# A gated mix of sliding-window attention and SwiGLU: values held in TensorE's four column strips while the exponentials stream

## Chip, cores and metric

One Trainium2 chip, one of its cores. The metric is the device time of one execution in microseconds (us), a median over runs. A profile is one execution, taken on its own.

## The reference, cut to what matters

Two branches over the same 2048 tokens of 512 numbers, mixed by a gate for each token: causal attention with a window of 256 keys and 32 heads of 16 numbers, and a SwiGLU feed-forward layer of width 1376. All inputs are bf16.

```python
qkv = (x @ wqkv).reshape(B, S, 3, H, Dh).transpose(2, 0, 3, 1, 4)   # H = 32, Dh = 16, S = 2048
q, k, v = qkv[0], qkv[1], qkv[2]
scores = jnp.einsum("bhqd,bhkd->bhqk", q, k) * (Dh ** -0.5)
mask = (idx[:, None] - idx[None, :] >= 0) & (idx[:, None] - idx[None, :] < 256)
p = softmax(jnp.where(mask, scores, -1e9))
a = jnp.einsum("bhqk,bhkd->bhqd", p, v).transpose(0, 2, 1, 3).reshape(B, S, D) @ wo
b = (silu(x @ w1) * (x @ w3)) @ w2
g = sigmoid((x * gate_w).sum(-1, keepdims=True))
out = g * a + (1 - g) * b
```

## The kernel before

**Order.** Nothing runs in source order. Every piece of work is an operation of a `Plan`, with an engine, an expected duration, inputs, a due time and the buffers that it takes and frees. `Plan.emit` (L62) is a list scheduler: it takes the engine that can start first, and among the operations that could start then the one that is due first; the instructions are then written out in that order. The attention stage's due times come from `at(c, t)`, which spreads 4 blocks of 16 steps over `TA` = 234.3 from `T0` = 11.49 (L292); the feed-forward's are spread evenly from `TF0` to `TF1` (L642). These numbers order the work and are no measurements. Each engine executes its list in order.

**Layout.** `xT` holds x transposed, 512 numbers in four chunks of 128 partitions. Attention runs in four blocks `c` of 8 heads (128 channels). A block's channels are four groups `s` of 32, two heads each; `a` or `h` names the head of a pair.

**Projections** (`projections`, L364): for each block and 512 tokens, K and Q as four 512-column matmuls each (L381), V as 128-column matmuls (L439). K is kept twice in `kbd`, each copy with the other head's rows set to zero by a multiplication with `rowsA`: in block 0 by VectorE and ScalarE out of PSUM (L390, L395), in the others by GpSimd out of the copy `kt` (L402, L405). A score tile so has 64 keys of head 0 and the same 64 keys of head 1 on its 128 partitions. V goes to `vbd` in four copies of half the partitions, two by ScalarE (L447) and two by VectorE (L449); each group's 34 columns are 16 values and a one for either head, with zeros elsewhere.

**Scores** (`main_batch`, L488, and `far_batch`, L515): a batch is 8 matmuls of 32 rows, in four row strips of TensorE, into `su`, four PSUM banks of which there is one set. ScalarE takes the exponentials of all four banks in one instruction (L505, L547, L553) into `E`. The diagonal is masked by VectorE (L486), the far edge of the window by GpSimd (L559). The pieces at the far edge of eight 64-key tiles are one batch.

**P times V** (`pv`, L576): for each 128 queries, a 128x128 piece of `E` is the weight and 34 columns of `vbd` stream, up to six pieces for each of four groups (L595). The result has the queries on partitions, 16 numbers and the sum beside them for each head. VectorE inverts the sums (L603), multiplies by them and by the gate `gq` (L606) into `oc`, and a transposing DMA on SP's queue (L612) writes it into `OT`.

**Output** (`output`, L795): four matmuls over `OT` and `wo` (L804), VectorE adds the feed-forward branch `bsb` (L816), which carries the factor 1 - g, and SP stores the row (L821). The last half row is summed on TensorE instead, by an identity matmul (L808).

**Feed-forward** (L658 on): gate and up matmuls (L712), a tanh on ScalarE (L722), two products on VectorE (L726, L732), the down matmuls (L773) and their eviction (L778).

**Start** (`opening`, L262): constants, 27 warm-up matmuls, x, then the weights, in the order in which they are issued; `landed` (L294) is when the plan expects them. x's first 512 tokens are transposed by TensorE (L319), the rest by transposing DMAs (L249). PSUM holds `su` and four banks `ch`, which everything else shares.

Of the kernel before, what the change touches and what calls it, by code (L numbers as in the profile page):

```python
# [13 lines left out]
DH = 16  # L14
# [7 lines left out]
class Op:  # L22
    __slots__ = ("eng", "dur", "lat", "fn", "deps", "due", "take", "free", "seq", "end", "slots")

    def __init__(self, eng, dur, fn, deps, due, take, free, lat, seq):
# [3 lines left out]
        self.end = None  # L29

# [8 lines left out]
class Plan:  # L39
# [22 lines left out]
    def emit(self):  # L62
# [14 lines left out]
        while ready:  # L77
# [21 lines left out]
            est, op = min(rows, key=lambda r: (r[1].due, r[1].seq))  # L99
# [25 lines left out]
def kernel(  # L125
# [27 lines left out]
    NKB = S // KB  # L153
    HALF = (0, 2, 4)
# [4 lines left out]
    ps = ctx.enter_context(tc.tile_pool(name="ps", bufs=1, space=bass.MemoryType.PSUM))  # L159

# [17 lines left out]
    kbd = pp.tile([P, NKB, 2, KB], BF16, name="kbd")  # L178
    qT = pp.tile([P, S + KB], BF16, name="qT")
    vbd = pp.tile([P, NKB, 4, 2 * (DH + 1)], BF16, name="vbd")  # L180
# [9 lines left out]
    mdiag = pp.tile([P, KB], BF16, name="mdiag")  # L190
    E = [pp.tile([P, 4, 4, 2, 384], BF16, name=f"E_{i}") for i in range(2)]
# [3 lines left out]
    oc = [pp.tile([P, 8, DH], BF16, name=f"oc_{i}") for i in range(8)]  # L195
    rden = [pp.tile([P, 8, 1], F32, name=f"rden_{i}") for i in range(8)]
# [3 lines left out]

    plan = Plan({"su": 1, "ch": 4, "E": 2, "kt": 2, "tt": 2, "h1": 2,
                 "oc": 8, "ot": 4, "hT": 1})
    add = plan.add


# [18 lines left out]
    def constants3():  # L224
        nc.gpsimd.memset(qT[:, S:S + KB], 0.0)
        nc.gpsimd.memset(mdiag[:], BIG)
        for lo in (0, KB):
            nc.gpsimd.affine_select(out=mdiag[lo:lo + KB, :], in_=mdiag[lo:lo + KB, :],
                                    pattern=[[1, KB]], compare_op=ALU.is_ge, fill=0.0,
                                    base=0, channel_multiplier=-1)  # L230

    def constants4():
        nc.gpsimd.memset(hb[:], 0.0)
        for e in E:
            nc.gpsimd.memset(e[:].rearrange("p t s a q -> p (t s) a q")[:, :, 0, 320:384], 0.0)
        v5 = vbd[:].rearrange("p k s (a d) -> p (k s) a d", a=2)
        nc.vector.memset(vbd[:, 0:NKB // 2], 0.0)
        nc.vector.memset(vbd[:, NKB // 2:NKB], 0.0)
        nc.gpsimd.memset(v5[0:KB, :, 0, DH:DH + 1], 1.0)
        nc.gpsimd.memset(v5[KB:P, :, 1, DH:DH + 1], 1.0)  # L240
# [21 lines left out]
    def opening():  # L262
# [10 lines left out]
        for b in (1, 0, 2):  # L273
            load_w(wqkv_sb, A_wqkv, b * D, b * D + 2 * P)
# [601 lines left out]
```

## Time and profile before

| | |
|---|---|
| median of 3 runs (lowest, highest) | 251.43 us (251.09, 251.58) |
| span of the profiled execution, first to last instruction | 249.4 us |
| TensorE busy | 244.4 us, 3483 matmuls |
| VectorE busy | 187.4 us |
| ScalarE busy | 185.4 us, of which L505 112.6 |
| GpSimd busy | 109.2 us, of which L559 65.0 and L405 37.6 |
| granted clock of TensorE, mean | 0.998 |
| first and last score batch start | 14.1 us and 236.7 us |

The span is what the engines did; the time of a run also has what lies before the first and behind the last instruction. A row of a group says which line, engine and operation, out<-in by the program's names, the shapes and how many; then the busy time and the mean in ns of one; then how long the engine stood idle just before them and what ended most of that. PE is TensorE, PEld its weight loads, DVE VectorE, ACT ScalarE, POOL GpSimd, and SPq the queue of SyncE that issues DMAs. A matmul's own duration includes its way through the array, so that matmuls overlap; the distance between the starts of two of them is what each takes of TensorE's line.

### The profile page before, as it was taken

Reading aid. Unit: us, or ns where it says so; the run is one execution under the profiler, and the core shown is the slowest. Engines: PE = TensorE matmul, PEld = TensorE weight load, DVE = VectorE, ACT = ScalarE, POOL = GpSimd, SP = SyncE. Lnnn points to the kernel's source line nnn. Section 1 sums busy time; section 2 is a strip of 40 time slices with the busy share of each in tenths; the row PEclk is TensorE's granted clock in tenths of the full one; section 3 lists DMA queues with packets and bytes.
Section 4 is the critical chain, followed back from the end, with each engine's and each line's share of the span. In section 5 each row is a group of like instructions: output and inputs, shape, how many; then the busy total and the mean of one; then the engine's idle time right before and its main releaser. Section 6 shows DMA issues by size and latency. Waiting matters only on the chain.

```text
span 249.4 us, 8138 instructions
## 1 busy us (share of the span) xinstructions
PE 244.4 (98%) x3483; PEld 133.8 (54%) x3483; DVE 187.4 (75%) x409; ACT 185.4 (74%) x186; POOL 109.2 (44%) x102
## 2 busy tenths in 40 slices
PE   8999999999999999999999999999999999999994
PEld 8645555555564554645464655555465554644462
DVE  5687888658878868757777988765787988787662
ACT  3377989688888887767888798776698877886631
POOL 8002945060318366475335717474344715470300
PEclk9999999999999999999999999999999999999999
DMA  6998951000000010100000010000000111211112
GB/s 202 314 253 251 230 136 25 16 8 13 13 5 18 13 26 11 20 8 11 13 8 18 5 25 19 20 5 13 13 5 18 29 38 45 61 50 54 51 53 75
DMA packets 30652, 13.67 MB, mean 55 GB/s; under 512 B 19896, under 2 KB 30616, under 8 KB 30616
## 3 DMA queue, kind: packets, MB, share of 16 engines
q1 hardware_dynamic: 29920, 12.70, 22.1%
q8 instruction: 27, 0.44, 0.8%
q10 hardware_dynamic: 696, 0.46, 0.6%
q14 instruction: 9, 0.07, 0.1%
HBM read 6.85 MB, written 2.10 MB: 36 GB/s over the span
## 4 chain that ended last, share of the span: by engine, by line
PE 94%; DVE 2%; DMA 1%; ACT 1%; issue 0%; SPq 0%; DVEq 0%
PE ch L712 29%; PE ch L773 15%; PE ch L595 15%; PE ch L381 11%; PE su L500 8%; PE ch L439 6%; PE ch L804 5%; PE su L532 2%; PE su L260 1%; DVE E L486 1%; DMA OT<-oc 1%; PE ch L672 1%; ACT E L505 1%; PE ch L319 1%; DVE oc L606 0%
## 5 line engine op out<-in xcount | busy, mean ns | idle before, releaser
L505 ACT ACTIVATE E<-su 128x2048 bf16<-128x2048 f32 x60 | 112.6, 1877 | 28.7 <-PE su L500 27.8
L559 POOL TENSOR_SCALAR_AFFINE_SELECT E<-E 64x1024 bf16<-64x1024 bf16 x56 | 65.0, 1161 | 84.7 <-ACT E L547 82.3
L712 PE MATMUL ch<-xT,w_sb 128*128 128x512 bf16 (+1 forms) x328 | 79.5, 375 | 0.0
L595 PEld LDWEIGHTS <-E 128*128 128x128 bf16 x1440 | 43.9, 96 | 12.8 <-issue 3.0
L405 POOL TENSOR_SCALAR kbd<-kt,rowsA 128x512 bf16<-128x512 bf16 x24 | 37.6, 1578 | 27.3 <-DVE kt L402 23.3
L595 PE MATMUL ch<-vbd,E 128*128 128x34 bf16 x1440 | 46.6, 178 | 0.5 <-DVE E L486 0.3
L712 PEld LDWEIGHTS <-w_sb 128*128 128x128 bf16 x328 | 28.3, 98 | 29.8 <-issue 3.6
L486 DVE TENSOR_TENSOR E<-E,mdiag 128x512 bf16<-128x512 bf16 x64 | 34.8, 544 | 9.1 <-ACT E L505 7.7
L773 PE MATMUL ch<-w_sb,hT 128*128 128x512 bf16 x160 | 41.3, 379 | 0.0
L726 DVE SCALAR_TENSOR_TENSOR h<-tt,ch 128x512 bf16<-128x512 bf16 (+1 forms) x44 | 30.1, 684 | 6.4 <-ACT tt L722 5.7
L381 PE MATMUL ch<-xT,wqkv_sb 128*128 128x512 bf16 x128 | 33.9, 379 | 0.0
L547 ACT ACTIVATE E<-su 128x2048 bf16<-128x2048 f32 (+1 forms) x16 | 26.6, 1663 | 8.9 <-PE su L532 6.5
L722 ACT ACTIVATE tt<-ch 128x512 bf16<-128x512 f32 (+1 forms) x44 | 26.0, 596 | 6.8 <-PE ch L712 6.3
L732 DVE SCALAR_TENSOR_TENSOR hT<-h,ch 128x512 bf16<-128x512 bf16 x40 | 27.5, 687 | 3.8
L603 DVE RECIPROCAL rden<-ch 128x8 f32<-128x8 f32 x64 | 13.1, 205 | 19.4 <-PE ch L595 18.8
L606 DVE SCALAR_TENSOR_TENSOR oc<-ch,gq,rden 128x128 bf16<-128x128 f32 x64 | 22.5, 351 | 2.3
L500 PE MATMUL su<-qT,kbd 32*128 32x256 bf16 x480 | 23.8, 273 | 0.0
L773 PEld LDWEIGHTS <-hT 128*128 128x128 bf16 x160 | 13.1, 97 | 13.0 <-issue 1.9
L500 PEld LDWEIGHTS <-kbd 32*128 32x128 bf16 x480 | 7.1, 92 | 22.1 <-issue 20.8
L439 PEld LDWEIGHTS <-xT 128*128 128x128 bf16 x256 | 15.5, 97 | 4.6 <-issue 1.5
L804 PE MATMUL ch<-wo_sb,OT 128*128 128x512 bf16 (+1 forms) x68 | 16.6, 367 | 0.3 <-DMA OT<-oc 0.3
L381 PEld LDWEIGHTS <-wqkv_sb 128*128 128x128 bf16 x128 | 10.7, 97 | 11.2 <-issue 1.7
(70 smaller groups left out, 167.8 us busy)
## 6 DMA issues: line engine op xcount, KB each, us to landing
out_dram<-ot SPq DMA_DIRECT2D x15, 128.0 KB, 1.9
wqkv_sb<-in_A_wqkv_dram SPq DMA_DIRECT2D x6, 256.0 KB, 5.3
w_sb<-in_B_w_dram SPq DMA_DIRECT2D x1, 1280.0 KB, 6.5
w_sb<-in_B_w_dram SPq DMA_DIRECT2D x2, 608.0 KB, 6.5
w_sb<-in_B_w_dram SPq DMA_DIRECT2D x2, 512.0 KB, 5.5
OT<-oc SPq DMA_TRANSPOSE x64, 2.3
wo_sb<-in_A_wo_dram SPq DMA_DIRECT2D x1, 512.0 KB, 5.0
xs<-in_A_x_dram SPq DMA_DIRECT2D x1, 256.0 KB, 2.8
```

What stands on the lines that cost most here:

```text
L381: nc.tensor.matmul(pst[:], lhsT=wqkv_sb[:, dc, col + c * P:col + (c + 1) * P], rhs=xT[:, dc, tq * 512:(tq + 1) * 512], start=(dc == 0), st ...
L405: nc.gpsimd.tensor_scalar_mul(out=kv[:, :, h, :], in0=kt[kj.at["kt"]][:].rearrange("p (k t) -> p k t", t=KB), scalar1=rowsA[:, h:h + 1])
L439: nc.tensor.matmul(pst[:, mm * w:(mm + 1) * w], lhsT=xT[:, dc, m * P:(m + 1) * P], rhs=rhs, start=(dc == 0), stop=(dc == NDC - 1))
L486: nc.vector.tensor_tensor(out=e, in0=e, in1=mdiag[:, None, :].to_broadcast([P, 8, KB]), op=ALU.min)
L500: nc.tensor.matmul(su[:, s, par * 256:(par + 1) * 256], lhsT=kbd[r, 2 * t + par, :, :].rearrange("p a k -> p (a k)"), rhs=qT[r, q0:q0 + 25 ...
L505: nc.scalar.activation(out=E[ej.at["E"]][:, t % 4, :, :, 0:256], in_=su[:].rearrange("p s (a q) -> p s a q", a=2), func=ACT.Exp, scale=SCALE)
L559: nc.gpsimd.affine_select(out=e[lo:lo + KB], in_=e[lo:lo + KB], pattern=[[0, 16], [-1, KB]], compare_op=ALU.is_ge, fill=0.0, base=-1, chan ...
L595: nc.tensor.matmul(po[:, 34 * s:34 * s + 34], lhsT=e[:, off:off + P], rhs=vbd[:, 2 * t + par, s, :], start=(bi == 0), stop=(bi == len(bloc ...
L712: nc.tensor.matmul(ch[job.at["ch"]][:, t0:t1], lhsT=wA[:, dc, :] if joint else w[:, dc, f * P:(f + 1) * P], rhs=xT[:, dc, tcb * 512 + t0:t ...
L726: nc.vector.scalar_tensor_tensor(out=h1[job.at["h1"]][ru, :], in0=tt[job.at["tt"]][rg, :], scalar=1.0, in1=ch[job.at["ch"]][rg, :], op0=AL ...
L773: nc.tensor.matmul(bps[:], lhsT=ht[:, mm * P:(mm + 1) * P], rhs=w2_sb[0:fs, f, :], start=(f == 0), stop=(f == NFC - 1))
L804: nc.tensor.matmul(pso[:, 0:part], lhsT=OT[:, c, m * P:(m + 1) * P], rhs=wo_sb[:, c, n0:n1], start=(c == 0), stop=(c == NDC - 1))
```

## The change

- **P times V is turned round.** V is the weight: 128 keys by 32 columns (16 values, the sum's column and padding) for one head, in one of four column strips of TensorE, one for each group of heads. The exponentials stream, up to 256 columns at a time. The two heads of a pair are two chains in two PSUM banks. `pv` runs for 512 queries at once: it waits for all their masks, and the result has channels on partitions, as `OT` needs them, without a transpose.
- **Scores are tiled by 128 keys of one head** (`head_keys`): 8 matmuls per main batch as before, over the 256 queries that start 64 behind the tile. The first 64 queries and the last 64 of four tiles are an edge batch. K has three copies: `kz` (zeros around the other head, `[h1 | h0 | h0 | h1]` by halves) and `k1`.
- **Masks**: GpSimd masks two 64x512 pieces per main batch (`near`, `far`), VectorE an edge batch in four instructions.
- **V** is copied out of PSUM by VectorE twice, and GpSimd makes four half copies of it for the edge tiles.
- **Softmax sums**: two DMAs gather them into `den`, VectorE inverts, two DMAs spill them to HBM, one spreads each over 16 partitions, four merge the second head's rows into `raw`; one product on VectorE writes `OT`. The gate moves to the output's eviction.
- **Start**: the first 512 tokens' K and Q weights are loaded ahead of w1 and w3, and K and Q come as two half chains each, where gate and up did before.
- **Order**: new due times (`K`), and ScalarE holds itself free for an exponential that will be ready soon (`hold`, negative here).

The core of the diff; flags beginning with `_` choose between placements, and `_pv` and `_vs` are set, `_km`, `_nm`, `_lo` are not.

```diff
-    T0, TA, TF0, TF1 = 11.49, 234.3, -7.168, 250.6
+    K = {"T0": 5.107, "TA": 219.856, "TF0": -3.263, "TF1": 261.659, "PV": -1.916, "EDGE": 1.036, "HOLD": -4.141, "LEAD": 11.653, ...}
+            held = [r for r in lists[eng] if r[1].hold and r[0] <= first + r[1].hold]
+            est, op = min(held or rows, key=lambda r: (r[1].due, r[1].seq))
...
+    vs = pp.tile([P, 2 * DH + 2, 3 * NV], BF16, name="vs")
+    Em = [pp.tile([P, 4, 2, 256], BF16, name=f"Em_{i}") for i in range(9)]
+    Ee = [pp.tile([P, 4, 4, 2, KB], BF16, name=f"Ee_{i}") for i in range(2)]
...
         load_x(0, 2, nc.sync)
         load_x(2, 4, nc.scalar)
-        load_w(w1_sb, B_w1, 0, 2 * P, True)
+        load_w(wqkv_sb, A_wqkv, D, D + 2 * P, True)
         nc.scalar.dma_start(out=gwr[:], in_=gate_w.rearrange("(c p) -> c p", p=P))
+        load_w(wqkv_sb, A_wqkv, 0, 2 * P)
+        load_w(w1_sb, B_w1, 0, 2 * P)
         load_w(w3_sb, B_w3, 0, 2 * P)
...
+            k_ready[(c, tq)] = [add("DVE" if K["_km"] else "POOL", 0.3 if K["_km"] else 1.6, lambda h=h: kmask(h), [b] + war, due, free=[(kj, "kt")])
+                                for h in range(3)]
...
+            def v_all(a, v_from=v_from, v_of=v_of):
+                nc.vector.tensor_copy(out=v_of(slice(0, P), 0, a), in_=v_from(slice(0, P), a))
+                    nc.gpsimd.tensor_copy(out=v_of(to, base, 0), in_=v_of(half, 0, 0))
+                nc.gpsimd.tensor_copy(out=v_of(rows, base, 1), in_=v_of(rows, 0, 1))
...
+            q0 = P * t + KB
+            for a in range(2):
+                for s in range(4):
+                    nc.tensor.matmul(su[:, s, a * 256:(a + 1) * 256], lhsT=head_keys(r, t, a),
+                                     rhs=qT[r, q0:q0 + 256], start=True, stop=True)
+        def near():
+            e = Em[job.at["Em"]][KB:P, :, :, 0:KB].rearrange("p s a q -> p (s a) q")
+            nc.gpsimd.affine_select(out=e, in_=e, pattern=[[0, 8], [1, KB]], compare_op=ALU.is_ge, fill=0.0,
+                                    base=0, channel_multiplier=-1)
...
+    def pieces_of(w):
+        q0, q1 = 512 * w, 512 * w + 512
+        res = []
+        for t in range(max(0, 4 * w - 2), 4 * w + 4):
+            lo, hi = max(q0, P * t + KB), min(q1, P * t + 320)
+            res.append(("main", t, lo, hi))
+            if t >= 4 * w:
+                res.append(("lo", t, P * t, P * t + KB))
+            if t < 4 * w + 2 and P * t + 320 < S:
+                res.append(("hi", t, P * t + 320, P * t + 384))
+        return res
+                for s in range(4):
...
+                    nc.tensor.matmul(po[32 * s:32 * s + 32, lo - 512 * w:hi - 512 * w],
+                                     lhsT=vs[:, 2 * a:2 * a + 32, i], rhs=mov, start=(n == 0),
+                                     stop=(n == len(todo) - 1), skip_group_check=True)
...
+        def gather(a):
+            (nc.scalar if final and a else nc.sync).dma_start(out=den[64 * a:64 * a + 64, :],
+                              in_=raw[DH - a:P:32, a, :].rearrange("p (r q) -> p r q", q=32))
+        def invert():
+            nc.vector.reciprocal(out=rden[:], in_=den[:])
+        def spill(a):
+            (nc.scalar if final and a else nc.sync).dma_start(out=hbm[:, a, :].rearrange("s (r q) -> s r q", q=32), in_=rden[64 * a:64 * a + 64, :])
+        def spread():
+            src = hbm[:].rearrange("s a q -> (s a) q")
+            nc.sync.dma_start(out=rec[:], in_=src[:, None, :].to_broadcast([8, DH, 512]))
+        def merge(s):
+            rows = slice(32 * s + DH, 32 * s + 32)
+            (nc.scalar if final and s % 2 else nc.sync).dma_start(out=raw[rows, 0, :], in_=raw[rows, 1, :])
         def norm():
-            nc.vector.scalar_tensor_tensor(out=oc[job.at["oc"]][:], in0=po8(job)[:, :, 0:DH],
+            (nc.gpsimd if K["_nm"] else nc.vector).tensor_tensor(out=OT[:, c, 512 * w:512 * w + 512], in0=raw[:, 0, :], in1=rec[:], op=ALU.mult)
...
-                nc.vector.tensor_tensor(out=dst, in0=ch[job.at["ch"]][:, 0:part],
-                                        in1=bsb[:, m, n0:n1], op=ALU.add)
+            nc.vector.scalar_tensor_tensor(out=ot[job.at["ot"]][:, 0:part], in0=ch[job.at["ch"]][:, 0:part],
+                                           scalar=gq[:, m:m + 1], in1=bsb[:, m, n0:n1],
+                                           op0=ALU.mult, op1=ALU.add)
```

More of the change, by code (lines that the diff above doesn't have):

```diff
@@ L364, in projections @@
     def projections(c, tq):
-        lead = 9.235 if c else 0.5758
+        lead = K["LEAD"] if c else 0.5758
         due = at(c, 4 * tq) - lead
@@ L563, in far_batch @@
[L563 to L569 removed]
+                        if q0 < S:
+                            keys, qs = kz[r, t, 2 * k:2 * k + 2, :].rearrange("p b x -> p (b x)"), q0
+                        else:
+                            keys, qs = head_keys(r, NT - 1, i - 2), S - KB
@@ new lines, in edge_batch @@
+        x = add("ACT", 1.86, ex, [a], due, free=[(job, "su")])
+        x.hold = HOLD
+        if K["_lo"]:
+            edge_ready[(c, h)] = [add("POOL", 1.16, lambda lo=lo: low(lo), [x], due) for lo in (0, KB)]
+            edge_ready[(c, h)].append(add("DVE", 1.09, high, [x], due - K["MK"]))
+        else:
+            edge_ready[(c, h)] = [add("DVE", 1.09, lambda half=half: mask(half), [x], due - K["MK"]) for half in range(2)]
+        if last:
+            main_ready[(c, NT - 1)] = []
+    def pieces_of(w):
[9 more added lines that the diff above has]
+        return res
@@ L639 @@
+        for w in range(NTC):
+            pv(c, w)
     ffn_total = NTC * ((NFC - 1) * 1.73 + 0.87 + 0.47 + 4 * 2.38)
```

452 lines of the change are left out of this document (242 added, 210 removed).

## The prediction

> **What bounds the kernel now.** The page comes first: its busy shares, the slices with the granted clock, and the chain of waits.
>
> ```profile
> span 249.4 us, 8138 instructions
> PE 244.4 (98%) x3483; PEld 133.8 (54%) x3483; DVE 187.4 (75%) x409; ACT 185.4 (74%) x186; POOL 109.2 (44%) x102
> PE   8999999999999999999999999999999999999994
> PEclk9999999999999999999999999999999999999999
> ...
> PE 94%; DVE 2%; DMA 1%; ACT 1%; issue 0%; SPq 0%; DVEq 0%
> ```
>
> TensorE is busy in every slice at full clock, and the chain that ended last lies 94% on it. A busy engine could still be an inefficient one, so the timeline of TensorE is read next: what counts is how long after a run's first matmul the next run starts.
>
> ```profile
> 100.12 0.76 PE L595 MATMUL ch<-vbd,E 128*128 128x34 bf16 x24
> 100.73 0.59 PE L773 MATMUL ch<-w_sb,hT 128*128 128x512 bf16 x2
> 101.16 0.38 PE L773 MATMUL ch<-w_sb,hX 96*128 96x512 bf16 x1
> 101.38 1.06 PE L439 MATMUL ch<-wqkv_sb,xT 128*128 128x128 bf16 x16
> 102.37 0.40 PE L500 MATMUL su<-qT,kbd 32*128 32x256 bf16 x8
> 102.70 0.60 PE L773 MATMUL ch<-w_sb,hT 128*128 128x512 bf16 x2
> ...
> 105.13 0.41 PE L532 MATMUL su<-qT,kbd 32*128 32x64 bf16 x32
> 105.48 0.60 PE L773 MATMUL ch<-w_sb,hT 128*128 128x512 bf16 x2
> ```
>
> A 512-column matmul takes 0.216 us of the line (100.73 to 101.16 for two), that is 2.4 columns per ns, with nothing between. A probability-times-V group of 24 (L595) takes 0.61 us, 25 ns each. A score group (L500) takes 0.33 us, and the run before it ends late: 16 matmuls of L439 need 0.89 us at their usual 56 ns and get 0.99, so entering the score group's four row strips costs some 0.10. Within the groups, four strips of 64 columns (L532) follow each other every 29 ns (27 is pure streaming), four of 256 every 119 (107). So TensorE is the bound: what is taken out of its line comes off the time, until something else ends later.
>
> The groups by line give the rest of the prices, and the DMA issues the landings:
>
> ```profile
> L505 ACT ACTIVATE E<-su 128x2048 bf16<-128x2048 f32 x60 | 112.6, 1877 | 28.7 <-PE su L500 27.8
> L559 POOL TENSOR_SCALAR_AFFINE_SELECT E<-E 64x1024 bf16<-64x1024 bf16 x56 | 65.0, 1161 | 84.7 <-ACT E L547 82.3
> L405 POOL TENSOR_SCALAR kbd<-kt,rowsA 128x512 bf16<-128x512 bf16 x24 | 37.6, 1578 | 27.3 <-DVE kt L402 23.3
> L595 PE MATMUL ch<-vbd,E 128*128 128x34 bf16 x1440 | 46.6, 178 | 0.5 <-DVE E L486 0.3
> L486 DVE TENSOR_TENSOR E<-E,mdiag 128x512 bf16<-128x512 bf16 x64 | 34.8, 544 | 9.1 <-ACT E L505 7.7
> L603 DVE RECIPROCAL rden<-ch 128x8 f32<-128x8 f32 x64 | 13.1, 205 | 19.4 <-PE ch L595 18.8
> L606 DVE SCALAR_TENSOR_TENSOR oc<-ch,gq,rden 128x128 bf16<-128x128 f32 x64 | 22.5, 351 | 2.3
> ...
> out_dram<-ot SPq DMA_DIRECT2D x15, 128.0 KB, 1.9
> OT<-oc SPq DMA_TRANSPOSE x64, 2.3
> ```
>
> **The change on TensorE.** Removed: 1440 matmuls of L595. From first start to the next line's first start, their 61 runs add up to 37.8 us. Added: per channel block and 512 queries, two chains (one per head of the pair), each of 14 pieces by four column strips (10 pieces for the first 512 queries, which have no earlier keys). Columns per chain: 1536 (1152 for the first), so 2 x (1152 + 3 x 1536) = 11,520 per block and 46,080 in all, if the four strips stream together. At 2.4 per ns: 19.2 us. The 416 quartets' own surcharge by the rows above (2 to 12 ns): 1.7. Entering and leaving strip mode, 0.10 each as at L500: 16 x 0.19 = 3.0 if the two chains stay together, 6.1 if other work comes between. Sum 24 to 27; I take 24.5, since both chains have the same due time and the same inputs. Gain 13.3. The final L808 matmul onto the branch sum goes, with the 0.44 that TensorE stood still behind it for the last transpose: -0.5. The last group is cut in four: +0.3.
>
> No row shows column strips, so this price needs both ends. Below: the row strips, as taken. Above: L595's 25 ns for each pair of a full 128-row weight load and its matmul. If the 1664 narrow loads, which also come from all 128 rows, follow each other at 25 ns, a quartet takes at least 100 ns (the 32 quartets of 256 columns: 107), 416 x 0.1 + 0.2 + 3.0 = 45 us: a loss of 7. Break-even is (37.8 - 3.0 - 19.2) / 416 = 37 ns per quartet above streaming, 9 per load. I take the low end: L532 also loads new weights for each 64-column matmul, 7 ns per pair, and L595 keeps four strips' columns in one load, so its 25 ns is no price for a quarter of them. Row strips share no rows, though, and that is the doubt.
>
> The Trainium skill (TensorE: Matmul & The Clock Gate, What overlaps and what doesn't, in The mechanism) says that a weight load overlaps running matmuls only where its row group differs, and column strips share all rows. Here the L773 run speaks against it: 0.216 us per 512 columns is streaming alone, though each has a 97 ns load in the same rows. The same page (Measured speedup vs the span model) gives 2.38x for three column strips; by that ratio streaming would cost 24 us in place of 19, an estimate.
>
> Score work is the same: 15 main batches of 8 x 256 columns and four of short pieces per block before and after. Start: K and Q of the first 512 tokens take the place of the two gate/up matmul pairs in quarter form; as many matmuls, loads of the same size in the same queue places, so TensorE starts the same (5.8 us). TensorE's sum: 249.4 - 13.3 - 0.5 + 0.3 = **235.9**, if it never waits.
>
> **Who else could end last.** ScalarE: V evictions go (13.3 us, L447's two forms) and the split of the last exponentials (4 x (2 x 1.02 - 1.88) = 0.6): 171 of 238. VectorE: minus 35.6 (L603, L606), plus 31 evictions x 0.69 = 21.3, 16 reciprocals of 32 columns at 0.21 to 0.40, and 16 products of 128x512 at 0.69 = 11: about zero net, 187, 79%. Its masks stay 64 of L486's size. L486 runs 0.42 us alone and up to 1.35 under a mask of L559; 17 of 64 were so held, which is the masks' 27% share of the time. GpSimd's masks grow to 77 us, 34%, but are half as long, so the loss stays near 8 us.
>
> GpSimd grows most. Masks: (1161 - 234)/960 gives 0.97 ns an element (the 64x64 mask took 234 ns), so 512 elements take 0.67, and 116 of them 77 us against 65. K: three writes per 512 tokens instead of two, 36 x 1.578 = 57 against 38; four plain copies 3. V: 48 copies at 0.40 and 32 at 0.29 (the L650 copies) = 29. Sum about 171, 72%. In a block after the first, per 512 queries of about 13.7 us: 7.25 x 0.67 + 3 x 1.58 + 4 x 0.40 = 11.2, 82%. If the strided V copies run at L405's 3.1 ns an element: 0.8 each, 12.8, 93%. Covered by the K work's lead of most of a period; without that cover the scores wait.
>
> SP loses 64 transposes at 1.1 us and gets 140 DMAs at about 0.5: 70 us each way. Queued behind a waiting `spread` (it waits for both spills to land) are the tail columns' transposes and output DMAs; behind a reciprocal or product waiting on VectorE, the evictions that free the four PSUM banks. If each of these 32 comes 0.3 us later than its place allows, that is up to 10 us of VectorE, which has 50 to spare; I charge 1.
>
> **The chain of scores.** One score buffer: batch to batch at least 2.76 us (0.33 + 0.12 until L505, 1.88, 0.43 back), median 2.985 now. The attention stage's due times are squeezed by 219.856/234.3, so I take 2.80. The first batch comes 3.1 us after the first K matmul is possible (now 9.61 for K, 12.7 for its last eviction), 8.9 to 9.5 against 14.08. The 76th: 9.2 + 75 x 2.80 = 219.2 (216.2 at the shortest). Then, in order: 0.45 + 1.88, mask 0.8, last pieces 0.4, eviction 0.8, gather 2.3, reciprocal 0.35, spill 2.1, spread 2.4, product 0.8, 16 output matmuls 3.5 (all four tiles now wait for the last product, before only two matmuls did), eviction 0.6, store 2.1: 18.5. End **237.7**; 234.7 at the shortest, 251 at today's median pace. Landings are those of the DMA rows. The 8 us of the four DMAs cost nothing while feed-forward work is left for TensorE; without it, up to 8.
>
> Both ends nearly coincide, and neither will meet exactly: span 238.5. Around the span lie 251.43 - 249.4 = 2.0 us: **240.5**.
>
> **Rivals.** (1) *The attention chain trails:* GpSimd near 93% delays K writes or masks, or the DMA round trip holds VectorE; batches keep 2.90 to 2.95. For it: one score buffer, 17 held masks, GpSimd at 82% by plan. Against: TensorE waits for almost nothing now, at VectorE's same load. End 9.2 + 75 x 2.92 + 18.5 = 246.7, 249 with what lies around; 245 where feed-forward work was held back: 246. (2) *Weight loads of the strips come one after another* at L595's pace: 235.9 + 45 - 24.5 = 256.4, so 258, slower from 9 ns per load on. For it: all loads read the same 128 rows. Against: L532's 7 ns. If loads hide behind no matmul at all, the quartet is 100 ns plus streaming: 19.2 + 41.6 + 3 = 64, and 277. By the skill's rule above it would be this. (3) *The strips do not stream together*, so the change does not do what it says: 4 x 19.2 + 1664 x 2.5 ns + 3 = 84, 297. Nothing speaks for it but that no row shows it. (4) The gain is used up by rival 1 and half of rival 2 together: no change.
>
> **Numbers.** Forecast 0.54 (own range 237.5 to 244.5), rival 1 0.22, rival 2 0.17 (0.04 of it at 277), rival 3 0.03, no change 0.04. The range runs from 237 (TensorE's sum is met nearly) to 253, which leaves out rivals 2 and 3. Within 0.2% no measurement of this kernel tells a change. Faster 0.54 + 0.22 and some of the fourth: 0.77; same 0.03; slower 0.20.
>
> **What would show it.** The column-strip group against the next line's start: 1.4 to 1.6 us for both chains; over 2.4 rival 2 is right. Score batches at 2.80 or at 2.9 and more. TensorE's first score near 9.2. GpSimd's share near 72%, V copies 0.4 or 0.8. Idle of TensorE before the last 16 output matmuls: none by the forecast. I am wrong if the strips cost more than L532 says, or if TensorE waits for `OT` at the end.

## The result, and the profile after

| | before | after |
|---|---|---|
| median (lowest, highest) | 251.26 us (250.99, 251.58) | 323.37 us (321.49, 326.84) |
| ratio, with its 95% interval | | 1.284 [1.277, 1.291] |
| span of the profiled execution | 249.4 us | 325.1 us |

The change makes the kernel 28% slower, where 240.5 us was forecast. The profiled execution is the longest of the four; the ratios, here and below, leave such slow executions out.

The page of after, in the order in which the page of before was read:

```profile
span 325.1 us, 8800 instructions
PE 261.9 (81%) x3698; PEld 143.0 (44%) x3738; DVE 211.1 (65%) x345; ACT 173.0 (53%) x142; POOL 230.2 (71%) x265
PE   8998939869495978869796959939797768959695
PEclk9999987979898799979987999987979799979989
...
PE 31%; DMA 27%; DVE 23%; issue 8%; ACT 4%; SPq 4%; DVEq 1%; ACTq 0%
```

No engine is full any more. TensorE's slices drop to 3 or 4 again and again, its granted clock falls with them, and the chain that ended last lies 27% on DMAs and 23% on VectorE, where it was 94% TensorE. So the question is no longer what TensorE has to do but what it waits for. Adding up the distances between matmul starts, and counting whatever a distance has over 0.3 us beyond streaming as a stall, TensorE's line of 320.3 us is 250.6 us of work and 69.7 us of stalls; in before it was 243.7 and 1.3. (Of after's 3738 matmuls 40 have no record in the trace; if all of them fell into stalls, 8.5 us of these were work.)

The groups, with shapes kept apart, show what became dear (columns as before: busy, mean ns of one | idle before it and what ended that):

```profile
L504 POOL COPY vs<-vs 64x256 bf16<-64x256 bf16 x24 | 32.8, 1367 | 1.0
L498 POOL COPY vs<-vs 64x256 bf16<-64x256 bf16 x24 | 32.5, 1354 | 10.6 <-DVE vs L492 9.6
L492 DVE CAST vs<-ch 128x256 bf16<-128x256 f32 x24 | 29.8, 1391 | 5.0 <-PE ch L477 4.7
L696 PEld LDWEIGHTS <-vs 128*32 128x32 bf16 x1664 | 42.2, 187 | 29.1 <-issue 20.9 <-DVE h L851 4.1 <-DVE vs L492 4.1
L744 DVE TENSOR_TENSOR OT<-xs,rec 128x512 bf16<-128x512 f32 x16 | 12.0, 752 | 57.8 <-DMA rec<-rd 40.4 <-DMA out_dram<-ot 5.9 <-issue 5.8
```

Two things stand out. Everything that writes or reads `vs` is about three times its forecast: half copies on GpSimd 1.36 us (0.40 forecast), evictions on VectorE 1.39, a load of 32 columns 187 ns, as much as two loads of 128 columns. And VectorE stands idle 57.8 us in front of one line, the 16 products L744, mostly until the spread sums `rec` land.

How such a wait reaches TensorE is seen in one stretch. First SyncE's queue, then VectorE, then TensorE (start and length in us, engine, line, operation, then how many):

```profile
162.23 1.19 SPq L726 DMA_DIRECT2D den<-xs  x2
164.04 2.46 SPq L741 DMA_DIRECT2D xs<-xs  x4
168.33 1.23 SPq L733 DMA_DIRECT2D rd<-rden  x2
170.83 0.64 SPq L737 DMA_DIRECT2D rec<-rd  x1
```

```profile
165.82 2.46 DVE L492 CAST vs<-ch 128x256 bf16<-128x256 f32 x2 [0.42 <-PE ch L477]
167.89 0.41 DVE L730 RECIPROCAL rden<-den 128x32 f32<-128x32 f32 x1
168.10 0.73 DVE L851 SCALAR_TENSOR_TENSOR h<-tt,ch 128x512 bf16<-128x512 bf16 x1
168.93 0.69 DVE L857 SCALAR_TENSOR_TENSOR hT<-h,ch 128x512 bf16<-128x512 bf16 x1
169.71 0.69 DVE L458 CAST qT<-ch 128x512 bf16<-128x512 f32 x1
174.45 0.69 DVE L744 TENSOR_TENSOR OT<-xs,rec 128x512 bf16<-128x512 f32 x1 [4.05 <-DMA rec<-rd]
175.06 0.68 DVE L851 SCALAR_TENSOR_TENSOR h<-tt,ch 128x512 bf16<-128x512 bf16 x1
```

```profile
172.76 0.28 PE L556 MATMUL su<-qT,k 32*128 32x256 bf16 x4
175.79 0.58 PE L837 MATMUL ch<-xT,w_sb 128*128 128x512 bf16 x1 [2.75 <-DVE h L851]
176.60 2.51 PE L837 MATMUL ch<-xT,w_sb 128*128 128x512 bf16 x6 [0.22 <-issue]
```

The sums are gathered at 162.23. The reciprocal comes at 167.89, behind two V evictions of 1.3 us each; the spills 168.33, the spread 170.83, the product 174.45. VectorE has nothing wrong with it in between: its queue holds the product next, and an engine that works in order does nothing until that can run. Behind it stands L851, which frees the PSUM banks of gate and up; TensorE runs out of banks at 173.0 and starts again at 175.79, when L851 is done. Then a second price follows: its six matmuls take 2.51 us, where the same six took 1.46 at 165.62. The windows show the granted clock at 1.00 until 175.3 us, at 0.50 from 175.3 to 178.7, and at 1.00 from there on. (The Trainium skill, TensorE: Matmul & The Clock Gate, What's actually happening, says that the clock falls to half after an idle window of about 3.4 us and comes back after a busy one of that length. The 3.4 us at 0.50 agree with the second; before the fall, TensorE had been idle for only 2.3 us, from 173.0 on.)

### The profile page after: what moved, and what is told of

The parts are those of the page before. It is cut to its first block, busy times and chain, and to the rows that moved or that the text cites. A ratio compares the mean times of both kernels' runs of the same rounds, so it can differ in the third digit from the quotient of the medians.

```text
span 325.1 us, 8800 instructions
## 1 busy us (share of the span) xinstructions
PE 261.9 (81%) x3698; PEld 143.0 (44%) x3738; DVE 211.1 (65%) x345; ACT 173.0 (53%) x142; POOL 230.2 (71%) x265
## 4 chain that ended last, share of the span: by engine, by line
PE 31%; DMA 27%; DVE 23%; issue 8%; ACT 4%; SPq 4%; DVEq 1%; ACTq 0%
DMA rec<-rd 13%; PE ch L696 11%; DMA rd<-rden 9%; DVE Ee L619 6%; DVE vs L492 6%; PE ch L917 5%; PE ch L837 4%; PE ch L887 3%; DVE h L851 3%; PE ch L403 3%; DVE OT L744 3%; PE su L556 3%; PE ch L477 2%; ACT Em L560 2%; DMA den<-xs 2%
## 5 line engine op out<-in xcount | busy, mean ns | idle before, releaser
L560 ACT ACTIVATE Em<-su 128x2048 bf16<-128x2048 f32 x60 | 112.7, 1878 | 95.8 <-PE su L556 93.2
L837 PE MATMUL ch<-xT,w_sb 128*128 128x512 bf16 x304 | 80.0, 392 | 14.4 <-DVE vs L492 5.5
L565 POOL TENSOR_SCALAR_AFFINE_SELECT Em<-Em 64x512 bf16<-64x512 bf16 x60 | 42.8, 714 | 40.0 <-ACT Em L560 36.9
L696 PE MATMUL ch<-Em,vs 128*32 128x256 bf16 (+2 forms) x672 | 41.8, 320 | 19.3 <-DVE vs L492 9.9
L696 PEld LDWEIGHTS <-vs 128*32 128x32 bf16 x1664 | 42.2, 187 | 29.1 <-issue 20.9
L498 POOL COPY vs<-vs 64x256 bf16<-64x256 bf16 (+1 forms) x40 | 45.1, 1126 | 11.7 <-DVE vs L492 10.0
L744 DVE TENSOR_TENSOR OT<-xs,rec 128x512 bf16<-128x512 f32 x16 | 12.0, 752 | 57.8 <-DMA rec<-rd 40.4
L504 POOL COPY vs<-vs 64x256 bf16<-64x256 bf16 (+1 forms) x40 | 45.3, 1133 | 1.7
L696 PE MATMUL ch<-Ee,vs 128*32 128x64 bf16 x992 | 42.0, 235 | 4.1 <-DVE Ee L619 4.1
L443 POOL TENSOR_SCALAR kz<-kt,rowsA 128x512 bf16<-128x512 bf16 x24 | 38.6, 1613 | 8.4 <-DVE kt L440 8.0
L492 DVE CAST vs<-ch 128x256 bf16<-128x256 f32 (+1 forms) x40 | 40.3, 1165 | 6.0 <-PE ch L477 4.7
L570 POOL TENSOR_SCALAR_AFFINE_SELECT Em<-Em 64x512 bf16<-64x512 bf16 x56 | 37.3, 667 | 3.3
L851 DVE SCALAR_TENSOR_TENSOR h<-tt,ch 128x512 bf16<-128x512 bf16 (+1 forms) x44 | 30.2, 687 | 6.3 <-ACT tt L847 6.1
L403 PE MATMUL ch<-xT,wqkv_sb 128*128 128x512 bf16 (+1 forms) x129 | 33.7, 377 | 0.4 <-issue 0.4
L917 PE MATMUL ch<-wo_sb,OT 128*128 128x512 bf16 (+1 forms) x65 | 18.3, 417 | 8.7 <-DVE OT L744 3.3
```

The lines of the kernel that those rows point to most:

```text
L403: nc.tensor.matmul(pst[:, t0:t1], lhsT=wqkv_sb[:, dc, col + c * P:col + (c + 1) * P], rhs=xT[:, dc, tq * 512 + t0:tq * 512 + t1], start=(d ...
L443: (nc.vector if K["_km"] else nc.gpsimd).tensor_scalar_mul(out=(kv0, kv1, k1v)[h], in0=by_half(kt[kj.at["kt"]][:]), scalar1=rowsA[:, min(h ...
L492: nc.vector.tensor_copy(out=v_of(slice(0, P), 0, a), in_=v_from(slice(0, P), a))
L498: nc.gpsimd.tensor_copy(out=v_of(to, base, 0), in_=v_of(half, 0, 0))
L504: nc.gpsimd.tensor_copy(out=v_of(rows, base, 1), in_=v_of(rows, 0, 1))
L560: nc.scalar.activation(out=Em[job.at["Em"]][:], in_=su[:].rearrange("p s (a q) -> p s a q", a=2), func=ACT.Exp, scale=SCALE)
```

## The experiments

Each has its edit against the kernel named, and its median and ratio to before. Where the expectations speak of a plan, they mean the sum of the durations that the kernel's own list scheduler holds: they order the work and measure nothing.

| label | edit | us | ratio [95%] |
|---|---|---|---|
| e1_packed_v | `vs` packed | 312.16 | 1.240 [1.235, 1.245] |
| e2_true_costs | measured durations in the plan | 314.1 | 1.248 [1.242, 1.254] |
| e3_packed_no_trip | e1, sums do not travel | 249.35 | 0.989 [0.986, 0.992] |
| e3s_strided_no_trip | the same, `vs` not packed | 286.31 | 1.139 [1.135, 1.143] |
| e4_packed_true_trip | e1, measured DMA times in the plan | 278.64 | 1.109 [1.102, 1.116] |
| b1_before_kq_first | before, K and Q loaded first | 252.81 | 1.006 [1.005, 1.008] |
| e6_landings_counted | e4, landings counted on one queue | 264.21 | 1.052 [1.048, 1.056] |
| e8_spread_by_tensor | e6, TensorE spreads the sums | 259.42 | 1.032 [1.027, 1.036] |
| e10_fitted | e8, late loads moved, part of the masks moved to GpSimd, due times fitted | 251.61 | 1.002 [1.000, 1.004] |
| e12_k_on_vector | e10, K writes on VectorE, due times fitted again | 251.73 | 1.000 [0.999, 1.002] |

### The prices by themselves (price)

A kernel of single loops, each timed from its first matmul to the first of the filling matmuls behind it.

> A kernel that computes nothing of the reference: it runs the disputed pieces by themselves, three or four times each, with full-array matmuls between so that TensorE's clock stays up. Theory 'stride' (V's 384-byte steps between neighbouring numbers make every reader and writer slow): 28 quartets of column strips of 64 columns take 2.5 us or more with strided weights and about 0.9 with packed ones; of 256 columns about 3.2 with both; GpSimd's half copy 1.3 us strided against 0.4 packed; VectorE's V eviction 1.3 against 0.45. Theory 'strip' (narrow weight loads follow each other at some 23 ns whatever the layout): 2.5 us both ways for 64 columns. One strip alone shows the load's own pace: 112 pairs at 25 ns or more. Row strips 28 x 29 ns = 0.8 us, the full-array group 48 x 25 ns = 1.2 us. The round trip of the sums through HBM: the forecast has 2.3 + 0.35 + 2.1 + 2.4 = 7.2 us from issue to product, the trace of the changed kernel suggests 8.5 or more.

Its timeline on TensorE, `vs` with neighbouring weights 384 bytes apart, `vc` with them side by side:

```profile
21.16 2.45 PE L64 MATMUL po<-xs,vs 128*32 128x64 bf16 x112 [4.61 <-DVE vs L126]
23.54 2.55 PE L59 MATMUL fl<-xs 128*128 128x512 bf16 x8
26.02 1.09 PE L69 MATMUL po<-xs,vc 128*32 128x64 bf16 x112
27.04 1.90 PE L59 MATMUL fl<-xs 128*128 128x512 bf16 x8
28.87 3.32 PE L74 MATMUL po<-xs,vs 128*32 128x256 bf16 x112
32.13 1.90 PE L59 MATMUL fl<-xs 128*128 128x512 bf16 x8
33.96 3.24 PE L79 MATMUL po<-xs,vc 128*32 128x256 bf16 x112
37.13 1.90 PE L59 MATMUL fl<-xs 128*128 128x512 bf16 x8
38.96 3.44 PE L83 MATMUL po<-xs,vc 128*32 128x64 bf16 x112
42.34 1.90 PE L59 MATMUL fl<-xs 128*128 128x512 bf16 x8
...
47.10 1.08 PE L92 MATMUL po<-xs 32*128 32x64 bf16 x112
48.12 1.90 PE L59 MATMUL fl<-xs 128*128 128x512 bf16 x8
```

28 quartets of 64 columns take 2.38 us strided (23.54 - 21.16), a little under the 2.5 expected, and 1.02 packed; the two repetitions of the strided loop took 2.98 and 2.70. Row strips (L92) take 1.02 as well: with packed weights, column strips cost the same. At 256 columns a quartet's streaming hides the layout, 3.26 strided and 3.17 packed. One strip alone (L83) takes 3.38, 30 ns a pair, so the strips do run beside each other. The forecast's doubt about column strips was unfounded, and its price held for weights laid out as L532's were. (The Trainium skill, TensorE: Matmul & The Clock Gate, What overlaps and what doesn't, lets a weight load overlap running matmuls only where its row group differs. All loads of the column strips use the same rows; 9 ns a pair in the packed loop speak against it.)

The same kernel gives a GpSimd copy of 64x256 as 1341 ns into `vs` and 458 into `vc`, and VectorE's eviction of 128x256 as 1460 and 466. One way of the sums, with nothing else on the queues: second gather issued 119.95, reciprocal 121.83, second spill 122.81, spread 124.65, product 128.69. So the spread takes 4.0 us from issue to use, where 2.4 was forecast.

### Packing the values (e1_packed_v), against after

```diff
-    vs = pp.tile([P, 2 * DH + 2, 3 * NV], BF16, name="vs")
+    vs = pp.tile([P, 3 * NV, 2 * DH + 2], BF16, name="vs")
...
-                                     lhsT=vs[:, 2 * a:2 * a + 32, i], rhs=mov, start=(n == 0),
+                                     lhsT=vs[:, i, 2 * a:2 * a + 32], rhs=mov, start=(n == 0),
```

> The changed kernel with the value tile's two free dimensions exchanged, so that a head's 16 values lie side by side; the same instructions in the same order. Theory 'stride': GpSimd's V copies fall from 1.1 to about 0.4 us and VectorE's evictions from 1.2 to 0.4, GpSimd's busy time by some 58 us to 172, VectorE's by 25; the strip groups fall from 2.6 to 1.6 us; the time comes to 245 to 255 us. Theory 'strip': copies as above, but the groups stay at 2.4 us or more, and the time is 262 to 272. Theory 'round trip' (VectorE waiting in order for the sums' way through HBM): the time stays above 290.

Measured 312.16 us. The prices fell to about what was forecast (groups of e1):

```profile
L504 POOL COPY vs<-vs 64x256 bf16<-64x256 bf16 x24 | 10.5, 436 | 1.9 <-DVE vs L492 1.0
L492 DVE CAST vs<-ch 128x256 bf16<-128x256 f32 x24 | 9.2, 415 | 3.2 <-PE ch L477 2.8
L696 PEld LDWEIGHTS <-vs 128*32 128x32 bf16 x1664 | 26.5, 108 | 25.1 <-issue 19.5 <-DVE h L851 3.6 <-DVE vs L492 1.3
L744 DVE TENSOR_TENSOR OT<-xs,rec 128x512 bf16<-128x512 f32 x16 | 11.4, 712 | 65.4 <-DMA rec<-rd 49.0 <-DMA out_dram<-ot 6.7 <-DMA hX<-hb 6.0
```

GpSimd has 173.5 us of work (171 forecast), VectorE 181.8 (187 forecast); a strip group that was not interrupted takes 1.47 us (1.4 to 1.6 forecast). Yet only 11 us came off, as the theory 'round trip' had it. VectorE has 29 us less to do and stands idle 14 us longer (309.9 - 181.8 = 128.1 us, in after 325.1 - 211.1 = 114.0); ahead of L744 its idle time rose from 57.8 to 65.4. The work of these two engines was not what set the end.

### Measured durations in the plan, layout kept (e2_true_costs), against after

```diff
-                prev = add("DVE", 0.42 if full else 0.28, lambda a=a, v_all=v_all: v_all(a), [prev], vdue,
+                prev = add("DVE", 1.36 if full else 0.82, lambda a=a, v_all=v_all: v_all(a), [prev], vdue,
...
-                    res.append(add("POOL", 0.4 if full else 0.28, lambda base=base, v_shift=v_shift: v_shift(base),
+                    res.append(add("POOL", 1.35 if full else 0.78, lambda base=base, v_shift=v_shift: v_shift(base),
...
-        b = add("SP", 0.45, spread, sp, due, take=[(cj, "rec")], lat=1.7)
+        b = add("SP", 0.64, spread, sp, due, take=[(cj, "rec")], lat=3.1)
```

(and the like for L504, the strips and the other DMAs.)

> The changed kernel with nothing but the plan's expected durations corrected to what its trace shows: V copies 1.35/0.78, V evictions 1.36/0.82, a strip group by 93 ns for each quartet, the spread of the sums 3.7 us; so only the order differs. Theory 'order' (the work would fit, but the plan placed waiting instructions ahead of ready ones): 280 to 295, most of TensorE's 70 us of idle gone. Theory 'stride' (GpSimd and VectorE are too slow whatever the order): above 305, since GpSimd's 228 us of work in the blocks after the first still fill its time.

Measured 314.1, above 305 as the theory 'stride' had it. VectorE's idle time ahead of L744 fell to 22.3 us, but TensorE's stalls only from 69.7 (61 at the least) to 54.3. The stalls moved: the strip groups' 64-column matmuls out of `Em` now stand behind 25.7 us of waiting, 18.3 of it for VectorE's `hT` products and V evictions. An order that knows these costs wins 9 us of 72. That no order could win more with this layout is not shown: this one was not fitted, and it has the error in counting landings that e6 mends.

### Without the way of the sums (e3_packed_no_trip, e3s_strided_no_trip)

Against e1 and against after, the same edit:

```diff
-        g = [add(queue(a), 0.45, lambda a=a: gather(a), [evs[a]], due, take=[(dj, "den")] if a == 0 else [], lat=1.5)
-             for a in range(2)]
-        r = add("DVE", 0.4, invert, g, due)
-        m = [add(queue(s % 2), 0.45, lambda s=s: merge(s), evs + [g[0]], due, lat=1.5) for s in range(4)]
-        sp = [add(queue(a), 0.45, lambda a=a: spill(a), [r], due, free=[(dj, "den")], lat=1.5) for a in range(2)]
-        b = add("SP", 0.45, spread, sp, due, take=[(cj, "rec")], lat=1.7)
-        ot_ready[(c, w)] = add("POOL" if K["_nm"] else "DVE", 1.3 if K["_nm"] else 0.6, norm, m + [b], due, free=[(rj, "raw"), (cj, "rec")])
+        m = [add(queue(s % 2), 0.45, lambda s=s: merge(s), evs, due, lat=1.5) for s in range(4)]
+        ot_ready[(c, w)] = add("POOL" if K["_nm"] else "DVE", 1.3 if K["_nm"] else 0.6, norm, m, due, free=[(rj, "raw")])
```

The merges stay, and no longer wait for a gather; `rec` is filled with ones at the start.

> As with packed V, and the division by the softmax sums left out: the sums' gather, inversion, spill and spread are gone, and the product multiplies by one. Against the packed kernel it shows what the round trip costs. Theory 'round trip': 20 us or more below the packed kernel. Theory 'stride': within 8 us of it, near what the plan's own order allows.

> The strided V of the changed kernel, and the division by the sums left out as before (product by one): the fourth corner of the square of 321 (strided, trip), 312 (packed, trip) and 249 (packed, no trip). Theory 'two causes that hide each other': strided alone costs far more than the 9 us that packing won, 20 to 45 us over 249, since GpSimd's 230 us and the dearer strip groups then decide. Theory 'trip alone': 250 to 260.

Four kernels now make a square:

| us | sums travel | sums do not travel |
|---|---|---|
| strided | 323.4 | 286.3 |
| packed | 312.2 | 249.4 |

The two costs do not add. Packing is worth 11 us while the sums travel and 37 when they do not; the way of the sums is worth 37 us with strided values and 63 with packed ones. Each covers for the other. The chain of e3s shows the cover when it is bared, its second line the lines that the chain lies on:

```profile
POOL 55%; PE 20%; DVE 7%; issue 7%; DMA 5%; ACT 3%; SPq 2%; DVEq 0%; ACTq 0%; POOLq 0%
POOL vs L505 12%; POOL vs L499 11%; POOL kz L444 11%; POOL Em L571 9%; POOL Em L566 8%; PE ch L833 5%; PE ch L697 5%; POOL k L444 4%; PE ch L883 3%; PE ch L913 3%; DMA w_sb<-in_B_w_dram 2%; DMA wqkv_sb<-in_A_wqkv_dram 2%; DVE vs L493 2%; ACT Em L561 2%; DVE Ee L620 2%
```

GpSimd, 82% busy, 91 us of it with the strided copies (L499, L505), sets the end there; in after no part of the chain lies on it. With both gone (e3) TensorE is back at 94%, with 231.1 us of work and 12.4 of stalls. This kernel lacks parts that the computation needs, so 0.989 is not a gain to be had; it is the nearest that the order of after comes to the forecast.

### The order alone (e4_packed_true_trip, against e1; e6_landings_counted, against e4)

e4 changes the expected durations of the way's operations: the issues of gathers, merges, spills and spread from 0.45 to 0.6 or 0.65, the spread's landing from 1.7 to 3.4, the product from 0.6 to 0.72. e6 changes one line of the scheduler:

```diff
-                    e = d.end if d.eng != op.eng else d.end - d.lat - SLACK
+                    e = d.end if d.eng != op.eng or d.lat > 1.0 else d.end - d.lat - SLACK
```

An operation on its input's own engine was taken to start when the input was issued. That is right for an engine; for two DMAs on one queue, where the spread needs the spilled bytes, it leaves out the landing.

> The packed kernel (312 us) with only the plan's expected durations of the sums' way corrected to the measured ones: gather and spill 0.6 us of the queue and 1.35 to 1.4 to land, merges 0.6, the spread 0.65 + 3.4 instead of 0.45 + 1.7, the product 0.72. Same work, another order. Theory 'early product' (VectorE executes in order and stands before each product because the plan expects the sums 3 us too early): the 65 us in front of the product shrink to under 15 and the time comes to 254 to 262 us. Theory 'traffic' (the round trip itself delays what needs it, whatever the order): above 285, since the single raw buffer and the last outputs still wait for it.

> The packed kernel with measured costs of the sums' way (279 us), and one line of the plan changed: where a DMA waits for another DMA of the same queue, the plan now counts the landing (it took two operations of one engine to follow each other without a wait, so the spread was planned right behind the spills, and the merges right behind the gather; the trace has the spread 1.24 us later than that each time, and the whole order slips by 1.2 us for each of the 16 groups). Theory 'early product': the rest of the loss goes too, the idle time in front of the product falls from 31 us to under 12, and the time comes to 262 to 268 us, which is what the plan expects (261.9) and what lies around. Theory 'traffic': it stays near 279.

The row of the product in e1 (65.4 us, above), e4 and e6:

```profile
L744 DVE TENSOR_TENSOR OT<-xs,rec 128x512 bf16<-128x512 f32 x16 | 12.0, 747 | 31.4 <-DMA rec<-rd 26.5 <-issue 4.8
```

```profile
L744 DVE TENSOR_TENSOR OT<-xs,rec 128x512 bf16<-128x512 f32 x16 | 12.3, 768 | 12.5 <-DMA rec<-rd 10.0 <-issue 1.8 <-DMA hX<-hb 0.6
```

e4 misses both of its ranges, since 31.4 us of the wait are left; e6 comes within its 262 to 268, with 12.5 us of the wait left where under 12 was expected. No operation is added or removed between e1 and e6, and 48 us are gone (312.16 to 264.21), while the idle time ahead of the product fell by 53. The sums do not come sooner: from the reciprocal to the product it takes 7.6 us in e1 and 8.7 in e6 (medians of 16). What changed is that the product stands later in VectorE's list, behind work that can run meanwhile: 11 instructions lie between the two in e6, 4 in e1 (medians). So these 48 of the 63 us were in-order waiting, and not the DMAs' work.

### The start alone (b1_before_kq_first), against before

K's and Q's first weights are loaded ahead of w1 and w3 and projected in half chains, as in the change. Due times are not fitted.

> The kernel before with only the change's start: K and Q weights loaded ahead of w1 and w3, K and Q of the first 512 tokens in two half chains, the same transposes' places, and due times as before. The forecast says nothing is won or lost on TensorE: 251 to 254 us (due times are not fitted to it, so 1 to 2 us may be lost), the first score batch near 10 us instead of 14.

The first score batch starts at 12.17 us instead of 14.08, not near 10 as expected, and the time is 0.6% longer, within the range. TensorE was full throughout before, so an earlier first batch had nothing to shorten.

### The sums spread by TensorE (e8_spread_by_tensor), against e6

```diff
-            src = hbm[:].rearrange("s a q -> (s a) q")
-            nc.sync.dma_start(out=rec[:], in_=src[:, None, :].to_broadcast([8, DH, 512]))
+            for r in range(16):
+                nc.tensor.matmul(ch[cj.at["ch"]][:, 32 * r:32 * r + 32], lhsT=sel[:, r, :], rhs=rden[:], start=True, stop=True)
```

The spills go too; `sel` holds 16 constant matrices of zeros and ones, and the inverted sums are bf16.

> As the kernel with landings counted, but the inverted sums are spread over their channels by 16 small TensorE matmuls with a selection matrix (bf16) into a PSUM bank, so that spill, HBM and spread are gone; gather, inversion and merges stay. Due times are not refitted. Theory 'early product': the way of the sums falls from 10 to about 4 us, TensorE pays 16 x 0.42 = 7 us, GpSimd and VectorE as in the packed kernel; 251 to 257 us. If the selection matmuls cost more than 25 ns each, or the merges and gathers alone still hold VectorE, 260 or more.

Measured 259.42: 5 us less than e6, and between the 251 to 257 of the theory and the 260 of the other case. TensorE stalls 20.0 us, in which up to 10 us of work may be counted (47 of 3994 matmuls have no record). The first gather waits behind the opening's last loads on SP's queue and lands at 38.9 us, for which VectorE stands 5.7 us.

### Loads moved, due times fitted (e10_fitted), and K on VectorE (e12_k_on_vector)

```diff
-        nc.sync.dma_start(out=wo_sb[:], in_=A_wo.rearrange("(c p) n -> p c n", p=P))
-        for b in (1, 0, 2):
-            load_w(wqkv_sb, A_wqkv, b * D + 2 * P, (b + 1) * D)
...
+    wo_in = add("SP", 2.6, late_loads, [arrive(K["LATE"])], K["LATE"], lat=6.0)
```

The fitted `K` also sets `_lo`, which the expectation does not name: in both runs GpSimd masks the first 64 queries of the edge batches, and VectorE only the last. Also, no gather is planned before 30 us. The due times of e12 are fitted anew.

> The kernel of e8_spread_by_tensor (values packed, inverted sums spread by TensorE, an order that counts landings) with two more edits: the opening's four late loads on SP's queue (wo and the rest of wqkv) become an operation with a due time of its own, since in that run the first gather stood behind them until 38.9 us and VectorE stood idle 5.7 us; and the due times are fitted anew, as the ones before were for a kernel of other durations. Theory (once values are packed and the sums no longer go through HBM, what is left of the loss is order, not work: TensorE's own work here is 233.5 us by the prices of e1 and e8 against 249.4 before): span 244 to 250, 246 to 252 us, ratio 0.98 to 1.00, TensorE idle in gaps over 0.3 us below 12 us. Rival A (four narrow column strips cost TensorE something that no plan can remove, beyond their price): still 256 or more, ratio 1.02 or more, with TensorE busy and not idle. Rival B (the sums' way still holds VectorE even without HBM: the gathers alone take 2 us each in 16 groups): 254 to 258, with VectorE's idle time in front of the reciprocal over 15 us.

> The kernel of e10_fitted, with the 36 masked K writes on VectorE instead of GpSimd and the due times fitted for that. In e10_fitted GpSimd is busy 213.2 of 249.7 us (85%, over 90% in most slices of the middle), its masks start up to 6 us behind their places in the order, and it stands for 40% of the chain of waits. Theory (what keeps that order from closing up is GpSimd: 36 x 1.6 us of K writes move to an engine at 68%): GpSimd's share below 65%, its part of the chain of waits under 15%, span 245 to 248, 247 to 250 us, ratio 0.983 to 0.995. Rival (TensorE's own sum plus its 5.8 us start is the bound there, and GpSimd only looks busy): GpSimd's share falls as much and the time does not, 250.5 to 253, ratio 0.997 or more.

Neither beats before: 251.61 and 251.73 us, ratios whose intervals run from 0.999 to 1.004. e10's stalls, 8.3 us, lie below the 12 of the theory, its span at the upper end, and the ratio of 0.98 to 1.00 is missed by a little. The 13 us of the forecast are there and are spent again. TensorE's line, by distances between starts:

| us | before | e10 | e12 |
|---|---|---|---|
| P times V | 37.4 | 23.0 | 22.1 |
| spreading the sums | | 6.5 | 7.6 |
| all else | 206.3 | 207.4 | 201.6 |
| stalls over 0.3 us | 1.3 | 8.3 | 14.6 |
| sum | 245.0 | 245.2 | 245.9 |

(In e12's trace 44 of 3994 matmul records are missing, so up to 9.4 us of its work may count as stalls; the sum holds.) In e10, 14.4 us are saved, 6.5 go into the selection matmuls, 7.0 into stalls. The second run was to say whether GpSimd keeps e10 from closing those stalls. Its load there is in part the fit's own doing: 178.0 us in e8, 213.2 in e10, with 37.6 of masks that were VectorE's in e8:

```profile
L633 POOL TENSOR_SCALAR_AFFINE_SELECT Ee<-Ee 64x1024 bf16<-64x1024 bf16 x32 | 37.6, 1174 | 4.1 <-ACT Ee L620 3.0
```

The busy lines and chains, e10 first:

```profile
PE 238.8 (96%) x3994; PEld 124.9 (50%) x3994; DVE 170.9 (68%) x301; ACT 172.3 (69%) x142; POOL 213.2 (85%) x300
...
PE 44%; POOL 40%; DMA 5%; DVE 3%; issue 3%; ACT 2%; SPq 1%; DVEq 0%; ACTq 0%; POOLq 0%
```

```profile
PE 235.1 (94%) x3950; PEld 127.2 (51%) x3994; DVE 188.2 (75%) x337; ACT 172.9 (69%) x142; POOL 159.2 (64%) x264
...
PE 74%; DVE 11%; DMA 5%; issue 5%; ACT 2%; SPq 2%; DVEq 0%; ACTq 0%
```

GpSimd left the chain (40% to nothing), and the time did not move, as the rival said. Its reason, that TensorE's own sum is the bound, is not shown: TensorE still stalls 8.3 us in e10, and at least 5 of the 14.6 in e12 are stalls. Since the order changed too, neither run says what a better order would win back.

## Why the prediction was wrong

**The way of the sums (the large error).** The forecast's step was: "If each of these 32 comes 0.3 us later than its place allows, that is up to 10 us of VectorE, which has 50 to spare; I charge 1." The size of the wait was wrong, 40.4 / 11 = 3.7 us for a product that waits for `rec`, up to 6.5, instead of 0.3, and so was the reason for forgiving it. An engine's spare time is no use while its next instruction waits; everything queued behind it waits too, here the evictions that free PSUM. VectorE stood 57.8 us there. Taking the way out of the packed kernel is worth 63 us; taking only the waiting out, by order (e1 to e6), 48. Smaller errors fed it: gather 2.3, reciprocal 0.35, spill 2.1 and spread 2.4 were laid end to end as 7.2 us, but the spread takes 4.0 by itself, the reciprocal stands behind other evictions, and four merges of 0.6 us each may stand on the queue ahead of the spills. The sentence "The 8 us of the four DMAs cost nothing while feed-forward work is left" failed for the same reason: there was feed-forward work, but its evictions stood behind the product.

**The layout of the values.** Three terms assumed that reading and writing `vs` costs what rows of packed tiles show: V copies 0.40 and 0.29 (measured 1.36 and 0.78, so 90 us instead of 29), V evictions at their old price (1.39 and 0.83), and the loads of the strips at L532's 7 ns. The upper bound of 0.8 per copy was too low as well. The diff shows the layout: the weights are `vs[:, 2*a:2*a+32, i]`, whose neighbours lie 3*NV = 192 elements apart. The forecast saw the stride at one place, the V copies, and took its bound for them from L405, whose elements lie side by side in runs of 64; at the evictions and the weight loads it did not price it at all. (The Trainium skill, SBUF — State Buffer, Door 1: The DMA port swizzle, says that SBUF is read in lines of 16 bytes, and that an access that goes to a new line each time pays for it; at 384 bytes every element does. The factor of three agrees in kind; the page gives no price.) Packed, all three terms came out close to the forecast.

**TensorE's strips.** Forecast 24.5 us of the line, after has 41.7: more than the 37.8 that it replaces. Packed, it is 22.7 to 23.0 (e3, e6, e10; where waits and a lower clock come in between, more: 29.0 in e1). So "Gain 13.3" was right for a layout that the change does not have. The measured groups of 2.6 to 3.1 us lie over the 2.4 at which the text would have called rival 2 right, and the strided loads do come at nearly its pace, 21 to 27 ns a pair in the price kernel. But its reason, that the loads read the same rows, is not the cause: packed weights read the same rows, at 9 ns a pair. (In that rival's sum, 32 quartets of 256 columns should be 64, which adds 0.2 us.)

**The chain of scores.** First batch forecast 9.2, measured 9.95; pace 2.80, median measured 2.86. The median holds and the last batch still starts at 297.5 instead of 219.2, because the stalls sit in a few long gaps that a median does not see. From the last batch to the end, 18.5 was forecast; after needs 27.6, e10 17.8.

**GpSimd and ScalarE.** Masks at 0.67 (measured 0.67 and 0.71), K writes at 1.58 (1.58 and 1.61), ScalarE at 171 (173): right.

**The rivals.** Rival 1 named the mechanism, "the DMA round trip holds VectorE", and priced it as a slightly slower pace, 246 us. What no row of before could give was the wait's size, since nothing there sends data through HBM and back in the middle of the work; but its bounds should have been taken from the whole way (in after 9.7 to 13.6 us from the second eviction to the product, 16 times), not from a share of it.

## What to carry to other kernels

Before pricing an instruction by a row of the same shape, read the strides of its operands in the code. And when a result travels through DMAs, price the wait at the place of its consumer in that engine's queue: the length of the way, minus the work that is queued ahead of the consumer, times the number of trips; spare time elsewhere on that engine doesn't count, and moving the consumer later in the list can be worth more than shortening the way. Two costs that hide each other need a square of four runs, since taking away either one alone shows only part of it.

## What the runs showed of the hardware that was not expected

- Column strips with packed weights of 32 columns cost as much as row strips: 112 pairs in 1.02 us either way.
- A distance of 384 bytes between neighbouring bf16 elements on both sides makes a GpSimd copy of 64x256 take 1341 ns instead of 458; on the written side it makes an eviction of 128x256 by VectorE take 1460 instead of 466, and on the read side a weight load of 128x32 192 instead of 94. At 256 streamed columns the slow load is hidden (3.26 against 3.17 us).
- A spread of 8 rows over 128 partitions out of HBM (256 KB written) takes 4.0 us from issue to use; its issue came 1.84 us after that of the spill whose bytes it needs.
- A masked K write of 128x512 takes GpSimd 1.56 to 1.75 us (e10, e3) and VectorE 0.44 to 0.54 (e12).
- In a stall of TensorE of 2.75 us, with a granted clock of 1.00 before it, the clock fell to 0.50 after 2.3 us and stayed there for 3.4 us, most of them busy.
